# One layer of gated attention and SwiGLU in one kernel: transfers, short tiles and operand pieces put in another order

## The chip, the cores and the metric

The kernel runs on one core of a Trainium2 chip. The core has five engines that run their own instruction queues: TensorE (PE, with PEld for its weight loads), VectorE (DVE), ScalarE (ACT), GpSimd (POOL) and SyncE (SP), which here issues transfers and order marks. The metric is the device time of one execution in microseconds; less is better. Times given for a kernel are the median of several executions; the profile is one execution, profiled by hardware.

## The reference

The input x has 2048 rows of D = 640. One half of the result is attention with a memory, in H = 32 heads of 20 columns, over N = 4 chunks ("segments") of L = 512 rows, one after the other; the other half is a SwiGLU feed-forward with F = 1728. A gate of each row mixes them.

```python
for s in range(N):
    logits = einsum("bhqd,bhkd->bhqk", qs, ks) * scale + mask     # causal, within the chunk
    a_dot = softmax(logits) @ vs
    pq = phi(qs)                                                  # phi(t) = t + 1 or exp(t)
    a_mem = (pq @ M) / (pq @ z + 1e-6)
    o = g * a_mem + (1 - g) * a_dot                               # g = sigmoid(beta), per head
    M, z = M + phi(ks).T @ vs, z + sum(phi(ks))
a = concat(o) @ wo
b = (silu(x @ w1) * (x @ w3)) @ w2
out = gate * a + (1 - gate) * b                                   # gate = sigmoid(sum(x * gate_w))
```

All arrays are float32. The kernel keeps that precision in most products by splitting an operand into a high and a low part and adding three products.

## The kernel before, in words

The work on TensorE is of two kinds. Attention is written out slot by slot: 40 slots for each quad of four heads, and in fixed slots the units `s` (scores, for the row maximum, `s_unit`), `t` (transposed scores, for the exponential, `t_unit`) and once a quad `o` (probabilities times v, `pv_quad`). Everything else is a stream of dense tiles, objects of class `Work`, that fills the time between the units: q, k and v projections, memory tiles (pm, pkt, nd), the feed-forward's gate and up tiles (g, u), its down tiles (f), the output projection (op) and its normalization (rr, gt). A name such as `f0_13_2_1` is kind, chunk, group or block, row block and half of the columns. A dense tile takes one of TensorE's eight result banks from its first matmul until its evacuation: f tiles are added to the accumulator `acc` by VectorE (L775) or, for the first group, written by ScalarE (L773); op tiles are added by VectorE (L1063).

A dense tile is computed in two halves, of rows 0 to 63 and of rows 64 to 127 of the array (`halves`). The two halves use separate parts of the array, so the second half of one tile runs beside the first half of a later tile. For an order between them, SyncE runs a nop when the first half's last matmul is done, and the second half's first matmul waits for it:

```python
        if r == 0 and i == len(todo) - 1 and w.todo[1]:
            w.seen = order(nc.sync.nop(), ins)
        if r == 1 and i == 0 and w.todo[0]:
            order(ins, w.seen)
```

This nop (L203 in the profile) is the "order mark" below. It stands in SyncE's queue in the order in which the program was written, and so behind the transfers that were written before it and behind what these wait for.

What sets the order: TensorE's and SyncE's instructions stand as they were written; a scheduler places those of VectorE, ScalarE and GpSimd. A list of segments (`seg`) gives the dense tiles of a stretch of attention; `braid` lets a side stream give a tile every so many nanoseconds of a modelled clock, `chain` joins streams, and `step` chooses at each time whether the next matmul is one of a first half (`under`) or of the oldest second half (`behind_one`, `flight`). `after(n, f)` runs `f` n slots later.

The places that matter here:
- The end of each chunk c. The attention sums go to memory as `od` (from `oq`, by ScalarE's queue); `o_sums` reads their denominators back as `rs` (L895), `o_load` reads the rest as `oall` (L909, L911), `o_scale` has VectorE take reciprocals and split them in three bfloat16 parts `rp` (L915 to L920), and six transfers spread them as `rR` (L924). Tiles rr multiply `oall` by them; gt adds the memory's part, and `oproj` splits `oall` into `oT` (high and low part, by `split`: ScalarE L129 and VectorE or GpSimd L130) for the op tiles.
- The feed-forward has 13 blocks of 128 columns and a half block of 64 (number 13), in groups of which the last is `[13, 12]`. A down tile of that group is short: ten matmuls with 320 columns. Up tiles end in `ft` (VectorE L746) and its split `ht` (ScalarE L129, GpSimd L130), which the down tiles take.
- Between chunks 1 and 2 the inputs X2 and X3 are split (`split_x`, ScalarE and VectorE), and q, k and v of chunks 2 and 3 are projected. Weights come as `wr` (SyncE L340) and are split into `W` (ScalarE L129, GpSimd L130).

## Time and profile before

| quantity | value |
|---|---|
| median of 3 executions | 1202.81 us (1202.58 to 1205.58) |
| the profiled execution | 1202.51 us, span 1200.6 us |
| TensorE busy | 1127.3 us, 94% of the span |
| VectorE, ScalarE, GpSimd busy | 582.7, 483.8, 550.7 us |
| mean granted clock of TensorE | 0.974 |

The span runs from the first to the last instruction on the core; the time of an execution is a little longer. A busy share is taken over the whole span, while each stretch of the program has its own limit, so the stretches and the waits tell more than the totals. In rows of the profile `out<-in` are the program's names without their numbers, `x` a count, and the name behind `<-` in a wait is what ended it. SPq is SyncE's queue, where transfers and order marks stand.

### The profile page before, as it was taken

Reading aid. Unit: us, or ns where it says so; the run is one execution under the profiler, and the core shown is the slowest. Engines: PE = TensorE matmul, PEld = TensorE weight load, DVE = VectorE, ACT = ScalarE, POOL = GpSimd, SP = SyncE. Lnnn points to the kernel's source line nnn. Section 1 sums busy time; section 2 is a strip of 40 time slices with the busy share of each in tenths; the row PEclk is TensorE's granted clock in tenths of the full one; section 3 lists DMA queues with packets and bytes.
Section 4 is the critical chain, followed back from the end, with each engine's and each line's share of the span. In section 5 each row is a group of like instructions: output and inputs, shape, how many; then the busy total and the mean of one; then the engine's idle time right before and its main releaser. Section 6 shows DMA issues by size and latency. Waiting matters only on the chain.

```text
span 1200.6 us, 29765 instructions
## 1 busy us (share of the span) xinstructions
PE 1127.3 (94%) x11798; PEld 994.9 (83%) x11798; DVE 582.7 (49%) x1719; ACT 483.8 (40%) x988; POOL 550.7 (46%) x737
## 2 busy tenths in 40 slices
PE   9999999999999999869899979978998899998798
PEld 6998989888889889759798758877887778886797
DVE  5032654445456534542245567552557464552544
ACT  5254345553442433533455524435443344344040
POOL 5344355565553444233444435544664447554040
PEclk9999999999999999988999999999999999999899
DMA  8365743333433234234477853425542434442112
GB/s 287 114 225 178 255 133 79 88 111 87 133 90 87 68 87 129 92 94 128 150 247 219 271 160 95 132 78 150 162 118 57 112 77 126 121 130 62 34 34 88
DMA packets 86125, 152.66 MB, mean 127 GB/s; under 512 B 20068, under 2 KB 33124, under 8 KB 85988
## 3 DMA queue, kind: packets, MB, share of 16 engines
q1 hardware_dynamic: 55908, 94.50, 24.0%
q0 software_dynamic: 22880, 41.86, 14.3%
q10 hardware_dynamic: 7200, 14.42, 3.2%
q8 instruction: 93, 1.52, 0.5%
q14 instruction: 44, 0.36, 0.1%
HBM read 95.25 MB, written 54.53 MB: 125 GB/s over the span
## 4 chain that ended last, share of the span: by engine, by line
PE 82%; DVE 7%; ACT 4%; DMA 3%; issue 2%; SPq 2%; POOL 0%; DVEq 0%; ACTq 0%; POOLq 0%
PE u L200 15%; PE f L200 15%; PE g L200 14%; PE o L878 6%; PE v L200 6%; PE op L200 5%; PE q L200 5%; PE k L200 5%; PE t L860 4%; PE s L824 3%; DVE junk L833 2%; SPq L924 1%; PE pm L200 1%; PE nd L200 1%; ACT P L865 1%
## 5 line engine op out<-in xcount | busy, mean ns | idle before, releaser
L200 PE MATMUL g<-X,W 64*128 64x512 f32 x1680 | 387.6, 398 | 0.4 <-SPq L203 0.4
L200 PE MATMUL u<-X,W 64*128 64x512 f32 x1560 | 374.4, 398 | 12.8 <-SPq L203 12.7
L833 DVE CUSTOM_DVE_ANT_0 junk<-s,mask 128x128 bf16<-128x128 f32 (+3 forms) x512 | 250.9, 490 | 217.8 <-PE s L824 180.0
L130 POOL TENSOR_TENSOR W<-wr,W 128x640 fp32r<-128x640 f32 (+1 forms) x126 | 196.8, 1571 | 216.4 <-ACT W L129 193.9
L200 PE MATMUL f<-W,ht 64*128 64x320 f32 x2624 | 278.8, 317 | 16.9 <-SPq L203 8.2
L200 PEld LDWEIGHTS g<-X,W 64*128 64x128 f32 x1680 | 270.5, 187 | 13.2 <-issue 1.8
L200 PEld LDWEIGHTS u<-X,W 64*128 64x128 f32 x1560 | 257.4, 187 | 28.7 <-SPq L203 13.5
L200 PEld LDWEIGHTS f<-W,ht 64*128 64x128 f32 x2624 | 258.4, 192 | 25.5 <-SPq L203 8.8
L865 ACT ACTIVATE P<-t 128x384 f32<-128x384 f32 (+1 forms) x384 | 181.1, 527 | 200.1 <-PE t L860 191.5
L868 POOL TENSOR_SCALAR_AFFINE_SELECT P<-P 128x256 f32<-128x256 f32 (+1 forms) x192 | 95.2, 499 | 304.9 <-ACT P L865 291.8
L129 ACT CAST W<-wr 128x640 fp32r<-128x640 f32 (+1 forms) x131 | 92.9, 726 | 88.5 <-PE f L200 30.0
L200 PE MATMUL op<-W,oT 64*128 64x320 f32 x960 | 105.9, 313 | 6.4 <-ACT oT L129 3.7
L860 PE MATMUL t<-qk 62*128 62x256 f32 (+2 forms) x512 | 98.0, 340 | 10.0 <-DVE m L833 3.1
L200 PEld LDWEIGHTS op<-W,oT 64*128 64x128 f32 x960 | 94.9, 187 | 10.9 <-ACT oT L129 5.6
L775 DVE SCALAR_TENSOR_TENSOR acc<-f,cgate,acc 128x320 f32<-128x320 f32 x128 | 69.8, 549 | 67.4 <-PE f L200 66.6
L200 PE MATMUL k<-X,W 64*128 64x512 f32 x600 | 100.5, 405 | 0.0
L824 PE MATMUL s<-qk 60*128 60x256 f32 (+2 forms) x512 | 91.7, 330 | 5.9 <-ACT acc L773 3.1
L200 PE MATMUL q<-X,W 64*128 64x512 f32 x540 | 95.6, 403 | 0.1
L200 PE MATMUL v<-W,X 64*128 64x320 f32 (+1 forms) x960 | 85.4, 312 | 4.3 <-ACT W L129 3.2
L200 PEld LDWEIGHTS v<-W,X 64*128 64x128 f32 x960 | 82.9, 189 | 5.4 <-ACT W L129 3.5
L130 POOL TENSOR_TENSOR ht<-ft,ht 128x512 fp32r<-128x512 f32 x52 | 67.2, 1292 | 39.6 <-ACT ht L129 39.3
L860 PEld LDWEIGHTS t<-qk 62*128 62x128 f32 x512 | 64.2, 187 | 22.1 <-DVE m L833 5.0
(116 smaller groups left out, 1306.9 us busy)
## 6 DMA issues: line engine op xcount, KB each, us to landing
qk<-qkd POOLq DMA_DIRECT2D x128, 240.0 KB, 3.8
wr<-in_w_dram SPq DMA_DIRECT2D x80, 320.0 KB
qkd<-qs SPq DMA_DIRECT2D x20, 512.0 KB
qkd<-ks SPq DMA_DIRECT2D x20, 512.0 KB
od<-oq ACTq DMA_DIRECT2D x32, 256.0 KB
wr<-in_wo_dram SPq DMA_DIRECT2D x20, 320.0 KB
vg<-vd SPq DMA_DIRECT2D x16, 336.0 KB
xr<-in_xT_dram SPq DMA_DIRECT2D x20, 256.0 KB
```

The costliest lines, as they stand in the source:

```text
L129: pin(nc.scalar.copy(dst[:, 0], src))
L130: (lo or nc.gpsimd.tensor_sub)(dst[:, 1], src, dst[:, 0].bitcast(F32))
L200: ins = nc.tensor.matmul(o, l, x, start=i == 0 and (r == 0 or not w.todo[0]), stop=i == len(todo) - 1 and (r == 1 or not w.todo[1]), skip_ ...
L775: nc.vector.scalar_tensor_tensor(dst, ps[:, :320], cgate[:, c, lb:lb + 1], dst, op0=ALU.mult, op1=ALU.add)
L824: nc.tensor.matmul(ps[i][:, o:o + n], q[:, qb * P:(qb + 1) * P], k[:, :n], start=qb != 1, stop=qb != 0, skip_group_check=True)
L833: nc.vector.tensor_tensor_reduce(out=junk[:, :n], in0=ps[i][:, o:o + n], in1=mask[:, L - n:], scale=1.0, scalar=-3.0e38, op0=ALU.add, op1= ...
L860: nc.tensor.matmul(ps[i][:, o:o + L - q0], k[:, kb * P:(kb + 1) * P], q[:, q0:], start=kb != 2, stop=kb != 3, skip_group_check=True)
L865: last["exp"] = nc.scalar.activation(u["P"][:, i, o:o + n], ps[i][:, b:b + n], AF.Exp, scale=SCALE)
L868: nc.gpsimd.affine_select(d, d, pattern=[[0, 2], [0, n], [1, P]], base=0, channel_multiplier=-1, compare_op=ALU.is_ge, fill=0.0)
L878: nc.tensor.matmul(ps[32 * i:32 * i + 32, kb * P:], heads[2 * p + i]["v"][:, kb], pairs[p + i // 2]["P"][:, i % 2, o:o + n], start=kb == 0 ...
L924: after(3 - i if c < NSEG - 1 else 2, lambda d=dst, s=rp[4 * h0:4 * h0 + 4 * n, i]: here(nc.sync.dma_start(d, s)))
```

## The change

The kernel does the same arithmetic. What differs is order:
- `rs`, `oall` and `rR` transfers of a chunk's end get slots of their own: one `oall` each second slot, `rR` from the third slot on, one a slot (for the last chunk one each second slot, and every second one of them goes to GpSimd's queue). `o_scale` follows `rs` after 8 slots instead of 10 (after 5 instead of 3 for the last chunk).
- A tile can name a condition (`ready`): a down tile, that `ht` exists; an op tile, that its `oT` exists. The stream holds tiles back in `waiting` until no first half is under way, and until no more than three second halves are left behind; otherwise `lower` runs matmuls of second halves alone. Sides and timed tiles, too, wait for fewer than three second halves.
- The last group of the feed-forward is cut by chunk: f0_13 runs as a side of u1 and then alternates with the splits of X2; the first four tiles of f1_13 run beside the store of chunk 0's result, the others as a side of v2, with X3's splits as another side. In the tail f2_13 stands right behind the up tiles, and op3 alternates with f3_13.
- `oT` is split in two pieces, of two and three blocks of 128 columns' length, instead of one.
- q's projections for the first block of chunks 2 and 3 come behind K's. Weights have a lower bound (`floors`), so that one still needed by the other chunk isn't given up.
- Stores of q, k and memory parts come a slot or two later; chunks 2 and 3 are stored block by block by `store_block`.

```diff
@@ step, pull
-                open_work(y)
+                waiting.append(y)
                 return True
...
+            elif n > 8 and lower():
+                return True
...
+    def lower():
+
+        if flight[0] is None:
+            dense["n0"] += APART
+            if not follow():
+                return False
+        w = flight[0]
+        if one(1, w):
+            flight[0] = None
+            close_work(w)
+        return True
...
-            elif dense["ns"] >= d.due and len(under) < 2:
+            elif dense["ns"] >= d.due and len(under) < 2 and len(behind_one) < 3:
...
-        elif under:
+        elif not under and waiting and (len(behind_one) > 3 or waiting[0].ready is not None and not waiting[0].ready()):
+            if not lower():
+                raise RuntimeError("nothing makes " + waiting[0].name + " ready")
+        elif under or waiting:
+            if not under:
+                open_work(waiting.popleft())
@@ ffn_down
-            return Work(f"f{c}_{js[0]}_{lb}_{hf}", parts, evac, 800, idx[0])
+            return Work(f"f{c}_{js[0]}_{lb}_{hf}", parts, evac, 800, idx[0], None, lambda: all((c, j) in hts for j in js))
@@ pv_quad, o_sums, o_load, o_scale
-            after(6 if c < NSEG - 1 else 2, o_sums, c)
+            after(6, o_sums, c)
...
-        after(10 if c < NSEG - 1 else 3, o_scale, c)
-        if c == NSEG - 1:
-            o_load(c, KB - 1)
-        else:
-            after(6, o_load, c, KB - 1)
+        after(8 if c < NSEG - 1 else 5, o_scale, c)
+        after(6 if c < NSEG - 1 else 2, o_load, c, KB - 1)
...
+        for i, (h, e, n, r) in enumerate(rows(b)):
+            src = od[c][h:h + n // DH, :DH] if n > DH else od[c][h, e:e + n]
+            after(1 + 2 * i, lambda d=oall[c][r:r + n, b], s=src: here(nc.sync.dma_start(d, s)))
...
+        end = c == NSEG - 1
         for i in range(3):
-            for base, h0, n in ((0, 0, R1H + 1), (64, R1H, H - R1H)):
+            for k, (base, h0, n) in enumerate(((0, 0, R1H + 1), (64, R1H, H - R1H))):
                 dst = rR[base + n * i:base + n * i + n].rearrange("h (a n) -> h a n", n=P)
-                after(3 - i if c < NSEG - 1 else 2, lambda d=dst, s=rp[4 * h0:4 * h0 + 4 * n, i]: here(nc.sync.dma_start(d, s)))
-        after(8, turned.append, c)
+                queue = nc.gpsimd if end and k else nc.sync
+                after(3 + 2 * i if end else 3 + 2 * i + k,
+                      lambda d=dst, s=rp[4 * h0:4 * h0 + 4 * n, i], q=queue: here(q.dma_start(d, s)))
+        after(11, turned.append, c)
@@ oproj
-            split(oT[0][:, qb % 2].rearrange("p a (b n) -> p a b n", n=P), oall[c][:, :, qb * P:(qb + 1) * P],
-                  lo=nc.vector.tensor_sub)
+            for b0, b1 in ((0, 2), (2, KB)):
+                split(oT[0][:, qb % 2].rearrange("p a (b n) -> p a b n", n=P)[:, :, b0:b1],
+                      oall[c][:, b0:b1, qb * P:(qb + 1) * P], lo=nc.vector.tensor_sub)
@@ the list of segments
+    def alternate(a, b):
+
+        def gen():
+            for y in a[1]:
+                yield y
+                z = next(b[1], None)
+                if z is not None:
+                    yield z
+            yield from b[1]
+        return a[0] + b[0], gen()
...
-    seg += [(0, load_raw(2)), (0, load_raw(3))] + u0 + [braid(chain(u1), (0, x2), 2800, 4500, False)]
-    d = job_down(A, 4)
-    q = job_q(B[:1], 0, {2: big_tile})
-    seg += [braid(chain([braid(braid(d, (0, store(0)), 2600, 12000), (0, x2), 5300)] + q), (0, x3), 4000, 13000)] + job_v(B)
-    seg += jobs_k(B) + job_q(B[1:], 0, {3: slot})
+    d0, d1 = jobs_down_by_chunk(A, 4)
+    v2, v3 = job_v(B)
+    seg += [(0, load_raw(2)), (0, load_raw(3))] + u0
+    seg += [braid(braid(chain(u1), (0, x2), 1900, 4200, False), d0, 2600, 2500, False), alternate(d0, (0, x2))]
+    seg += [braid(take(d1, 4), (0, store(0)), 700), braid(braid(v2, d1, 2400), (0, x3), 3000, 2000), v3]
+    seg += jobs_k(B)
+    q = job_q2(B, 0, {2: big_tile, 3: slot})
+    seg += q[:2]
...
-    tail = [braid(chain([d] + u), o1, 1500, 10500)] + [o2, job_down(B, 4, True)]
+    tail = [braid(chain([d] + u + [d2]), o1, 1500, 10500), alternate(o2, d3)]
```

VectorE's order where the short down tiles of chunk 0 are evacuated (`acc0<-f0_13_...`; X2 is the split of chunk 2's input, junk and m are row maxima of attention, fu and ft are of an up tile). Before:

```order
L775 SCALAR_TENSOR_TENSOR acc0_2778<-f0_13_0_0_7610,cgate_101,acc0_2778 128x320
L307 TENSOR_TENSOR X2_7512<-xr2_7245,xh2_4_7724 128x512
L775 SCALAR_TENSOR_TENSOR acc0_2778<-f0_13_0_1_7629,cgate_101,acc0_2778 128x320
L775 SCALAR_TENSOR_TENSOR acc0_2778<-f0_13_1_0_7649,cgate_101,acc0_2778 128x320
L775 SCALAR_TENSOR_TENSOR acc0_2778<-f0_13_1_1_7659,cgate_101,acc0_2778 128x320
L775 SCALAR_TENSOR_TENSOR acc0_2778<-f0_13_2_0_7669,cgate_101,acc0_2778 128x320
L307 TENSOR_TENSOR ns0_98<-m48_7084,nh24_7797 128x16
L844 STREAM_TRANSPOSE mr_7801<-ns0_98 32x32 x4
L775 SCALAR_TENSOR_TENSOR acc0_2778<-f0_13_2_1_7679,cgate_101,acc0_2778 128x320
L775 SCALAR_TENSOR_TENSOR acc0_2778<-f0_13_3_0_7701,cgate_101,acc0_2778 128x320
L775 SCALAR_TENSOR_TENSOR acc0_2778<-f0_13_3_1_7717,cgate_101,acc0_2778 128x320
```

And now, from the third of these tiles on:

```order
L758 SCALAR_TENSOR_TENSOR fu1_12_7666<-ft1_12_7665,g1_12_7492 128x512
L809 SCALAR_TENSOR_TENSOR acc0_2776<-f0_13_1_0_7603,cgate_101,acc0_2776 128x320
L775 SCALAR_TENSOR_TENSOR ft1_12_7665<-fu1_12_7666,u1_12_7586 128x512
L809 SCALAR_TENSOR_TENSOR acc0_2776<-f0_13_1_1_7649,cgate_101,acc0_2776 128x320
L869 ISA junk_7752,m48_7132<-s25_2_0_7748,mask_85 128x512
L869 ISA m48_7132 128x1
L869 ISA junk_7754,m48_7132<-s25_2_1_7749,mask_85 128x512
L869 ISA m48_7132 128x1
L809 SCALAR_TENSOR_TENSOR acc0_2776<-f0_13_2_0_7678,cgate_101,acc0_2776 128x320
L809 SCALAR_TENSOR_TENSOR acc0_2776<-f0_13_2_1_7690,cgate_101,acc0_2776 128x320
L809 SCALAR_TENSOR_TENSOR acc0_2776<-f0_13_3_0_7710,cgate_101,acc0_2776 128x320
L809 SCALAR_TENSOR_TENSOR acc0_2776<-f0_13_3_1_7730,cgate_101,acc0_2776 128x320
```

Before, the tiles stood one behind the other; now two steps of the up tile 12 of chunk 1 and row maxima of another pair lie among them, and X2's split has moved ahead.

VectorE's order at the end of chunk 2, up to where `o_scale` makes `rp` from `rs`. Before:

```order
L775 SCALAR_TENSOR_TENSOR acc3_11984<-f3_3_3_0_13511,cgate_101,acc3_11984 128x320
L833 ISA junk_13650,m100_13360<-s51_0_0_13644,mask_85 128x128
L833 ISA m100_13360 128x1
L833 ISA junk_13652,m100_13360<-s51_0_0_13644,mask_85 128x256
L833 ISA m100_13360 128x1
L833 ISA junk_13654,m100_13360<-s51_0_1_13645,mask_85 128x128
L833 ISA m100_13360 128x1
L833 ISA junk_13656,m100_13360<-s51_0_1_13645,mask_85 128x256
L833 ISA m100_13360 128x1
L915 RECIPROCAL rs_95<-rs_95 128x128
L775 SCALAR_TENSOR_TENSOR acc3_11984<-f3_3_3_1_13554,cgate_101,acc3_11984 128x320
```

And now:

```order
L809 SCALAR_TENSOR_TENSOR acc3_12012<-f3_3_2_1_13478,cgate_101,acc3_12012 128x320
L945 RECIPROCAL rs_95<-rs_95 128x128
L946 TENSOR_SCALAR rs_95<-rs_95,cR_93 128x128
L947 CAST rp_96<-rs_95 128x128
L869 ISA junk_13653,m100_13355<-s51_0_0_13647,mask_85 128x128
L869 ISA m100_13355 128x1
L948 TENSOR_TENSOR rs_95<-rs_95,rp_96 128x128
L869 ISA junk_13655,m100_13355<-s51_0_0_13647,mask_85 128x256
L869 ISA m100_13355 128x1
L949 CAST rp_96<-rs_95 128x128
```

The reciprocal stood behind the evacuation of f3_3_3_0 and the first row maxima of pair 51 (s51); now it stands ahead of both, right behind f3_3_2_1.

SyncE's order at the end of chunk 3, from `rs` on (order marks are not among these rows). Before:

```order
L895 DMA rs_95<-od3_79 128x1x128
L911 DMA oall3_15601<-od3_79 8x512
L909 DMA oall3_15601<-od3_79 120x1x512
L924 DMA rR_97<-rp_96 20x4x128
L924 DMA rR_97<-rp_96 13x4x128
L924 DMA rR_97<-rp_96 20x4x128
L924 DMA rR_97<-rp_96 13x4x128
L924 DMA rR_97<-rp_96 20x4x128
L924 DMA rR_97<-rp_96 13x4x128
L340 DMA wr128_16430<-in_wo_dram 128x640
```

And now:

```order
L931 DMA rs_95<-od3_79 128x1x128
L941 DMA oall3_15616<-od3_79 8x512
L941 DMA oall3_15616<-od3_79 120x1x512
L957 DMA rR_97<-rp_96 20x4x128
L369 DMA wr127_16445<-in_wo_dram 128x640
L957 DMA rR_97<-rp_96 20x4x128 x2
L369 DMA wr128_16506<-in_wo_dram 128x640
L369 DMA wr129_16874<-in_wo_dram 128x640
```

Three of the six `rR` are left here, with loads of wo between them; the other three stand in GpSimd's queue. At the end of chunk 2 the six still stand one behind the other among SyncE's transfers.

87 lines of the change are left out of this document (55 added, 32 removed).

## The prediction

> **What bounds the kernel now.** I read the page first, for the span and for who is busy, then the stretches of 20 to 30 us, to find where TensorE does less than elsewhere, then TensorE's waits, and last the queue of SyncE and the chain at each hole.
>
> ```profile
> span 1200.6 us, 29765 instructions
> PE 1127.3 (94%) x11798; PEld 994.9 (83%) x11798; DVE 582.7 (49%) x1719; ACT 483.8 (40%) x988; POOL 550.7 (46%) x737
> ```
>
> The second line makes TensorE the bound, and no other engine is busy for half of the span. Since the change leaves all matmuls in place, it can only win what TensorE loses. In the stretches below (start:end, length, then busy us and number of instructions for PE, PEld, DVE, ACT, POOL, then the granted clock) I compare numbers of matmuls, since a busy PE may be a slow one.
>
> ```profile
> 360.00:380.00 20.00, 18.70 (x236) 17.70 (x235) 13.96 (x43) 3.14 (x8) 4.44 (x8) 1.00 0.23 68
> 390.00:420.00 30.00, 30.00 (x306) 25.32 (x304) 16.37 (x48) 12.46 (x24) 13.67 (x13) 1.00 0.24 69
> 450.00:480.00 30.00, 30.00 (x380) 28.61 (x380) 14.76 (x41) 9.44 (x20) 14.78 (x20) 1.00 0.45 126
> 480.00:510.00 30.00, 26.17 (x231) 23.50 (x219) 16.11 (x46) 14.86 (x27) 8.64 (x8) 0.94 0.28 95
> 510.00:540.00 30.00, 20.36 (x171) 16.97 (x171) 13.94 (x30) 12.06 (x23) 10.71 (x17) 0.83 0.32 94
> 540.00:570.00 30.00, 28.95 (x343) 27.19 (x345) 8.50 (x33) 9.04 (x23) 9.18 (x16) 0.89 0.40 124
> 690.00:720.00 30.00, 22.47 (x206) 17.40 (x204) 17.69 (x55) 8.30 (x17) 10.93 (x15) 0.91 0.50 160
> 720.00:750.00 30.00, 29.98 (x291) 24.55 (x289) 21.13 (x63) 14.30 (x31) 16.91 (x23) 0.98 0.33 91
> 750.00:780.00 30.00, 30.00 (x357) 25.66 (x356) 16.86 (x55) 12.32 (x26) 17.45 (x27) 1.00 0.51 135
> 780.00:810.00 30.00, 23.98 (x270) 21.08 (x268) 16.23 (x58) 9.90 (x20) 12.12 (x16) 0.94 0.25 74
> 810.00:840.00 30.00, 26.91 (x304) 23.74 (x304) 8.96 (x37) 16.09 (x34) 12.98 (x23) 0.94 0.51 148
> 920.00:940.00 20.00, 13.49 (x114) 11.70 (x111) 11.52 (x35) 7.00 (x15) 7.60 (x9) 0.83 0.31 93
> 1110.00:1120.00 10.00, 2.92 (x22) 2.92 (x24) 2.99 (x8) 0.62 (x1) 2.62 (x2) 0.69 0.15 36
> ```
>
> Full stretches give the price of a matmul: 30.00/380 = 79 ns where the short ones (64x320) prevail, 30.00/306 = 98 ns and 29.98/291 = 103 ns where the long ones (64x512) do, 30.00/357 = 84 ns for a mixture. Length less number times price is what each hole loses:
> - A, 480 to 570 (the short down projection of chunks 0 and 1): 30 - 231 x 0.098 = 7.4, 30 - 171 x 0.079 = 16.5, 30 - 343 x 0.079 = 2.9: 26.8 us.
> - B, 690 to 720 (end of chunk 1): 30 - 206 x 0.103 = 8.8.
> - C, 780 to 840 (output projection of chunk 1, then f2_0): 60 - 574 x 0.084 = 11.8.
> - D, 920 to 940 (end of chunk 2): 20 - 114 x 0.103 = 8.3.
> - E, 1110 to 1120 (end of chunk 3): 10 - 22 x 0.079 = 8.3.
> - end of chunk 0, 360 to 380: 20 - 236 x 0.079 = 1.4.
>
> Together 65.4 us. TensorE's waits (total, times, longest) say what ends them:
>
> ```profile
> PE u L200 <- SPq L203: 12.7, 3, 6.5
> PE f L200 <- SPq L203: 8.2, 2, 8.0
> PE f L200 <- DVE acc L775: 5.0, 5, 2.1
> PE op L200 <- ACT oT L129: 3.7, 7, 0.7
> PE s L824 <- ACT acc L773: 3.1, 1, 3.1
> PE op L200 <- DVE oT L130: 2.7, 6, 1.1
> ```
>
> The first two are TensorE waiting for SyncE's order mark (the nop between a tile's halves), which stands in SyncE's queue behind transfers. They are B, D and E. The third is A: 16 tiles of ten matmuls in all eight banks, each opened when VectorE has emptied an old one.
>
> **The change part by part.** Spaced transfers first. SyncE's timeline and the chain show what it stands behind at each end:
>
> ```profile
> 368.25 5.23 SPq L924 DMA_DIRECT2D rR<-rp  x6
> 705.49 0.58 SPq L895 DMA_DIRECT2D rs<-od  x1
> 927.85 5.07 SPq L924 DMA_DIRECT2D rR<-rp  x6
> 1111.83 5.13 SPq L924 DMA_DIRECT2D rR<-rp  x6
> ```
> ```profile
> 699.18 6.29 DMA od<-oq
> 807.06 8.34 DMA wr<-in_w_dram
> 1107.06 3.18 DMA rs<-od
> ```
>
> One rR costs 5.07/6 = 0.85 us of SyncE's time. At the end of chunk 3 (E) the order of after puts one rs, one oall and then an order mark, and the rR come singly, with three given to GpSimd. So neither the landing of rs nor the six issues stand before the marks of f2_9. Of 8.3 us I take 8.0, since one issue of 0.85 can still show; bounds 6 (a mark behind two transfers and a cold clock) and 9 (the slow matmuls around it too). GpSimd's three issues stand among its splits of wo's weights, which aren't asked for before the tail: at nothing, but without that cover the weights, and op with them, come 3 x 0.85 us later. At D all six rR are still together in SyncE's order, but VectorE's scaling, for which SyncE stands at this end today, comes some 2 us of TensorE's work sooner, and the mark behind the six, of u2_6, is needed 5.5 us after the one ahead. (Distances in TensorE's work are counted in the orders: matmuls between, times the prices above.) 6 x 0.85 = 5.1 just fits, and the fifth is needed by the normalization matmul. I take 6 of 8.3, bounds 3 and 8. At B three rR stand ahead of the mark of u3_0 instead of two, but VectorE's scaling comes earlier; rs still waits for the 6.29 us of od's landing, which nothing in the change shortens. I take 3 of 8.8, bounds 0 and 7. End of chunk 0: the 5.23 us are spread over several marks, 1.0 of 1.4, bounds 0 and 1.4.
>
> Short tiles, A. In the order of after the second halves stay about four tiles behind instead of seven, and other tiles, x2's splits and v2 lie between. A bank is then asked for 0.9 to 1.8 us of TensorE's work after its VectorE step begins, which the 0.55 us below fits into. What is late next is the first tile of each set: f0_13 opens right behind u0_12, f1_13 behind u1_12, so each waits for the three steps that make ht (line, engine, operation, tiles; busy us, mean ns):
>
> ```profile
> L129 ACT CAST W<-wr 128x640 fp32r<-128x640 f32 (+1 forms) x131 | 92.9, 726 | 88.5 <-PE f L200 30.0 <-PE u L200 23.1 <-PE op L200 12.9
> L746 DVE SCALAR_TENSOR_TENSOR ft<-fu,u 128x512 f32<-128x512 f32 x52 | 35.6, 685 | 30.7 <-PE u L200 30.2
> L129 ACT CAST ht<-ft 128x512 fp32r<-128x512 f32 x52 | 32.3, 621 | 55.3 <-DVE ft L746 53.2 <-DMA od<-oq 2.1
> L130 POOL TENSOR_TENSOR ht<-ft,ht 128x512 fp32r<-128x512 f32 x52 | 67.2, 1292 | 39.6 <-ACT ht L129 39.3
> L775 DVE SCALAR_TENSOR_TENSOR acc<-f,cgate,acc 128x320 f32<-128x320 f32 x128 | 69.8, 549 | 67.4 <-PE f L200 66.6
> ```
>
> 0.685 + 0.621 + 1.292 = 2.6 us. Between lie 0.6 us of work for f0_13 (2.0 late) and 1.5 for f1_13, where one cast of a weight (0.726) stands ahead on ScalarE (1.8 late). Such a stall also slows what follows:
>
> ```profile
> 502.27 0.38 PE L860 MATMUL t<-qk 62*128 62x256 f32 x1 [2.13 <-DVE m L833]
> 504.79 0.62 PE L200 MATMUL u<-X,W 64*128 64x512 f32 x1
> 506.37 0.39 PE L200 MATMUL u<-X,W 64*128 64x512 f32 x1
> ```
>
> After 2.13 us without work a matmul takes 0.62 instead of 0.39 us until 506.4, so four us at little over half speed: at most 2 us lost, at least none; I take 1.2 for a stall of two. New losses 2.0 + 1.8 + 2 x 1.2 = 6.2, and 2 more for v's weights and x3's splits, which share the engines: 26.8 - 8.3 = 18.5 gained. Bounds 8 (half of the lock-step stays with the new stalls) and 24. The Trainium skill, "TensorE: Matmul & The Clock Gate", section "Why this matters for your kernels", sets the limit for keeping the full clock at idle gaps of about 3 us. By that rule stalls of 2 us cost no clock, and three of them would be 3.6 us cheaper, 1158 instead of 1162; the row of 502.27 speaks against it, with the reservation that another short wait follows there.
>
> q behind K moves q's first projections of chunks 2 and 3 behind the K tiles. The matmuls are the same; their stores come to SyncE's queue later, and the load of pair 16 that reads them stands 12 us of TensorE's work behind. Another 12 are left till the first s unit, which cover the landing below: at nothing; without that cover the unit waits for a load, 3.8 us.
>
> ```profile
> qk<-qkd POOLq DMA_DIRECT2D x128, 240.0 KB, 3.8
> ```
>
> Operand in pieces. A piece of 256 or 384 columns takes less than the whole 640, so the first op matmul waits for roughly half as long; the waits are 3.7 + 2.7 = 6.4 us. In the tail op3 and f3_13 also alternate, which gives each piece a tile's time. I take 4.5, bounds 2 and 6.4; the 32 added casts and subtractions lie on engines that are idle for half of the span. Against it stands the tail's new first tile: f2_13 follows u2_12 after 0.15 us of work, so 2.6 - 0.15 = 2.4 late and 1.2 of clock. Net 0.9, bounds -1.6 and 5. C also holds a weight that comes late (8.34 us in flight, with ScalarE's cast ahead of the evacuations that TensorE's s unit waits 3.1 us for). That cast's place hardly moves, so I take 3 of 11.8, bounds 0 and 8. The limit on sides (a memory tile only when fewer than three halves are behind) and the later store slots move work that has slack: nothing.
>
> Sum: 18.5 + 3 + 3 + 6 + 8 + 0.9 + 1.0 = 40.4. The profiled execution took 1202.51, as good as the median of 1202.81: 1202.5 - 40.4 = 1162. The low ends sum to 8 + 0 + 0 + 3 + 6 - 1.6 + 0 = 15 (1187), the high ones to 24 + 7 + 8 + 8 + 9 + 5 + 1.4 = 62 (1140).
>
> **Rivals.**
> The stalls only move. If ht's three steps and the dense VectorE keep A at its low end, the tail too, and B and C give nothing: 8 + 6 + 8 - 1.6 + 1 = 21, 1181. For it speaks that A's tiles, splits and ht share three engines; against, that VectorE is busy for 13.94 of 30 us there.
> All holes close: 1140. For it, that every hole has an edit; against, od's 6.29 us and the weight's 8.34, which none shortens.
> The spacing isn't there: the six rR stay together at the ends of chunks 1 and 2, and if the marks still fall behind them, B and D give nothing: 40.4 - 9 = 31.4, 1171. The order speaks for it, the marks' places against it.
> Slower: the scaling of the sums (o_scale) comes two slots sooner, and VectorE works in order.
>
> ```profile
> DVE rs L915 <- DMA rs<-od: 3.3, 1, 3.3
> ```
>
> If its reciprocal is now reached while rs is in flight, VectorE stands, and all evacuations with it. The longest flight would be od and rs, 6.29 + 0.58 + 3.18 = 10 us. At four chunk ends that is 40 us, and the gains at the ends (18) don't come: 1202.5 - 22.4 + 40 = 1220. It decides from 22.4/4 = 5.6 us a stop. Against it: today VectorE stands there once, for 3.3 us, with TensorE idle anyway.
>
> **How the numbers follow.** My forecast (1152 to 1170) has 0.40, the moved stalls 0.20, the missing spacing 0.12, all holes closed 0.15, the stop of VectorE 0.10, and 0.03 is left for gains and stops that cancel. A change is measurable from 0.3%, 3.6 us: faster 0.87, same 0.03, slower 0.10. The range 1141 to 1188 takes in the bounds and all but the last two cases.
>
> **What would show it.** After: no wait of u or f for the order mark over 2 us at the ends of chunks 2 and 3; A's stretches with over 300 matmuls in 30 us and no row of five waits for acc; instead two or three waits of f for ht near 2 us, one in the tail; op's waits under 3 us. The prediction fails if VectorE waits for rs more than 5 us an end, if a new wait for weights or qk appears in A, or if C's late weight costs more than now.

## The result and the profile after

| kernel | median | lowest to highest | against before |
|---|---|---|---|
| before | 1202.81 us | 1202.58 to 1205.58 | |
| after | 1165.18 us | 1160.91 to 1166.93 | 0.9673 (95%: 0.9627 to 0.972) |

The change wins 38 us. The profiled execution of after took 1166.93 us, the longest of its three. The page's first lines, as for before:

```profile
span 1165.2 us, 29806 instructions
PE 1113.2 (96%) x11798; PEld 993.9 (85%) x11798; DVE 584.9 (50%) x1735; ACT 485.8 (42%) x1003; POOL 551.4 (47%) x739
```

TensorE ran the same 11798 matmuls and was busy for 14 us less; its mean granted clock was 0.990 instead of 0.974. Some stretches of after, with the columns of the prediction's stretches (by the milestones below, the same work stands 5 us later than before at A, 13 us earlier at B and 19 us earlier at D):

```profile
480.00:510.00 30.00, 24.31 (x218) 20.15 (x216) 13.90 (x31) 14.59 (x26) 9.99 (x10) 0.97 0.43 135
510.00:540.00 30.00, 26.89 (x288) 24.71 (x287) 16.16 (x42) 13.33 (x29) 14.99 (x25) 0.92 0.34 98
540.00:570.00 30.00, 30.00 (x404) 28.33 (x402) 10.77 (x42) 10.88 (x30) 5.72 (x9) 1.00 0.31 105
690.00:720.00 30.00, 26.50 (x243) 22.24 (x241) 19.40 (x62) 11.26 (x23) 17.36 (x25) 1.00 0.56 153
900.00:920.00 20.00, 19.18 (x172) 15.35 (x173) 13.60 (x40) 8.15 (x17) 12.55 (x17) 1.00 0.53 128
1080.00:1090.00 10.00, 8.81 (x114) 8.53 (x112) 6.99 (x13) 1.35 (x2) 5.00 (x6) 1.00 0.37 101
```

The two holes behind the order marks, D (now from 900 on) and E (now near 1085), are nearly closed: 172 matmuls in 20 us and 114 in 10, where before held 114 and 22. B (690 to 720) is smaller. A is the surprise: at 510 the count rose from 171 to 288, but 480 to 510 holds 218 where before held 231. TensorE's waits in after (total, times, longest):

```profile
PE t L896 <- ACT acc L807: 3.3, 2, 2.9
PE f L201 <- POOL ht L130: 3.3, 3, 1.6
PE f L201 <- ACT ht L129: 2.8, 2, 1.4
PE pm L201 <- SPq L204: 2.4, 1, 2.4
PE f L201 <- DVE acc L809: 2.2, 2, 1.2
PE op L201 <- DVE oT L130: 1.9, 2, 1.4
PE g L201 <- SPq L204: 1.7, 1, 1.7
```

The 12.7 and 8.2 us for order marks are gone. Of the five waits of f for acc two are left, both far behind the short tiles (at 886 and 1010); among the short tiles an s unit now waits for acc instead, 1.8 us at 507. The waits of f for ht are the first tiles of the short sets. Two waits for an order mark are new: that of a memory tile (pm) in the head, and that of a gate tile (g) in A. At the end of chunk 2 the six rR still come together in SyncE's queue, and VectorE's wait for rs is small:

```profile
904.29 5.44 SPq L957 DMA_DIRECT2D rR<-rp  x6
```
```profile
DVE rs L945 <- DMA rs<-od: 5.4, 2, 3.5
```

To see where the time went I use a milestone that all kernels share: the start of ScalarE's copy of a quad's attention sums. There are 32 of them, eight a chunk, counted from 0, and the quads' attention is the same in all kernels, so the time between two of them goes by the dense tiles woven in. Two such rows of after, of quads 9 and 12:

```profile
443.52 0.59 ACT L919 COPY oq<-o 128x512 f32<-128x512 f32 x1 [2.81 <-PE o L914]
589.32 0.59 ACT L919 COPY oq<-o 128x512 f32<-128x512 f32 x1 [4.62 <-PE o L914]
```

Their difference, 145.8 us, is the second line of this table; the other lines are worked out in the same way, and the last column is what the prediction had for the holes that lie there.

| stretch | what it holds | before | after | gained | predicted |
|---|---|---|---|---|---|
| to quad 9 | head, end of chunk 0 | 438.5 | 443.5 | -5.0 | 1.0 |
| 9 to 12 | A, the short tiles | 152.7 | 145.8 | 6.9 | 18.5 |
| 12 to 15 | K, q and memory tiles of chunks 1 to 3 | 107.4 | 96.5 | 10.9 | nothing |
| 15 to 16 | B, end of chunk 1 | 33.4 | 28.7 | 4.7 | 3 |
| 16 to 23 | C, op of chunk 1, f2_0 | 181.4 | 180.2 | 1.2 | 3 |
| 23 to 24 | D, end of chunk 2 | 32.3 | 26.2 | 6.1 | 6 |
| 24 to 31 | op of chunk 2, feed-forward | 158.7 | 155.6 | 3.1 | part of 0.9 |
| from 31 | E, end of chunk 3, the tail | 96.2 | 88.7 | 7.5 | 8, part of 0.9 |
| sum | span | 1200.6 | 1165.2 | 35.4 | 40.4 |

A tile that was moved can change stretches, so the first three don't hold quite the same work. TensorE's matmuls and mean granted clock in them, before and after:

| stretch | matmuls before | after | clock before | after |
|---|---|---|---|---|
| to quad 9 | 4480 | 4506 | 1.00 | 1.00 |
| 9 to 12 | 1486 | 1498 | 0.93 | 0.98 |
| 12 to 15 | 976 | 931 | 0.97 | 1.00 |

At some 0.1 us a matmul, for the same work the head lost about 2.4 us instead of 5.0 (pm's new wait is 2.4), the short tiles gained about 8 instead of 6.9, and the stretch from 12 to 15 about 6.4 instead of 10.9.

The ends of the chunks came out near the forecast. The short tiles gave 7 or 8 of 18.5, and a place where the prediction saw nothing gave 6 to 11.

### The profile page after: what moved, and what is told of

Same layout as the page of the kernel before. It is cut to its first block, busy times and chain, and to the rows that moved or that the text cites. A ratio compares the mean times of both kernels' runs of the same rounds, so it can differ in the third digit from the quotient of the medians.

```text
span 1165.2 us, 29806 instructions
## 1 busy us (share of the span) xinstructions
PE 1113.2 (96%) x11798; PEld 993.9 (85%) x11798; DVE 584.9 (50%) x1735; ACT 485.8 (42%) x1003; POOL 551.4 (47%) x739
## 5 line engine op out<-in xcount | busy, mean ns | idle before, releaser
L201 PE MATMUL g<-X,W 64*128 64x512 f32 x1680 | 383.2, 397 | 2.5 <-SPq L204 1.7
L201 PE MATMUL u<-X,W 64*128 64x512 f32 x1560 | 363.6, 397 | 1.8 <-ACT P L901 1.0
L201 PEld LDWEIGHTS g<-X,W 64*128 64x128 f32 x1680 | 266.5, 186 | 14.4 <-SPq L204 2.1
L201 PEld LDWEIGHTS u<-X,W 64*128 64x128 f32 x1560 | 253.7, 186 | 13.2 <-issue 2.0
L201 PE MATMUL q<-X,W 64*128 64x512 f32 x540 | 88.6, 396 | 0.0
L201 PE MATMUL v<-W,X 64*128 64x320 f32 (+1 forms) x960 | 82.7, 307 | 0.6 <-DVE acc L809 0.6
L201 PEld LDWEIGHTS k<-X,W 64*128 64x128 f32 x600 | 80.7, 187 | 2.2 <-issue 0.2
```

Source lines behind the costliest of these rows:

```text
L201: ins = nc.tensor.matmul(o, l, x, start=i == 0 and (r == 0 or not w.todo[0]), stop=i == len(todo) - 1 and (r == 1 or not w.todo[1]), skip_ ...
```

## The experiments

Twelve kernels were run, each timed against before on the same chip. All compute the whole result. The first table has their times; the second, from the one profiled execution of each, the length of six stretches in us. The profiles scatter with the executions (old_short and tail_order, whose instructions are the same up to there, differ by 4.5 us between quads 18 and 20), so the second table tells places, and the first one sizes.

| kernel | median us (range) | against before (95%) |
|---|---|---|
| old_transfers | 1190.79 (1189.38 to 1192.57) | 0.990 (0.9843 to 0.9956) |
| only_transfers | 1181.34 (1179.84 to 1183.47) | 0.9822 (0.9766 to 0.9878) |
| old_short | 1151.9 (1150.74 to 1152.45) | 0.9574 (0.9509 to 0.9638) |
| one_piece | 1172.26 (1170.99 to 1177.46) | 0.9753 (0.9694 to 0.9812) |
| no_limit | 1183.09 (1180.93 to 1187.52) | 0.9825 (0.98 to 0.985) |
| only_limit | 1178.79 (1176.91 to 1182.87) | 0.9789 (0.9767 to 0.9811) |
| old_short_q | 1164.42 (1160.68 to 1169.48) | 0.9667 (0.9632 to 0.9703) |
| combined | 1159.35 (1156.87 to 1160.55) | 0.962 (0.9604 to 0.9637) |
| tail_order | 1146.29 (1140.33 to 1150.6) | 0.9521 (0.9475 to 0.9566) |
| combined_held | 1158.72 (1157.68 to 1159.34) | 0.9625 (0.9585 to 0.9664) |
| limit_transfers | 1159.23 (1158.24 to 1159.69) | 0.9631 (0.9598 to 0.9663) |
| combined_vector | 1156.13 (1153.51 to 1159.92) | 0.9584 (0.9542 to 0.9626) |

| kernel | to 9 | 9 to 12 | 12 to 15 | 15 to 16 | 23 to 24 | from 31 |
|---|---|---|---|---|---|---|
| before | 438.5 | 152.7 | 107.4 | 33.4 | 32.3 | 96.2 |
| after | 443.5 | 145.8 | 96.5 | 28.7 | 26.2 | 88.7 |
| old_transfers | 443.7 | 145.1 | 96.6 | 33.5 | 36.9 | 96.3 |
| only_transfers | 436.1 | 151.5 | 107.5 | 28.7 | 27.0 | 88.7 |
| one_piece | 444.3 | 146.5 | 96.6 | 28.6 | 26.2 | 88.8 |
| no_limit | 443.4 | 153.4 | 102.5 | 28.4 | 30.1 | 88.8 |
| only_limit | 437.9 | 138.7 | 107.5 | 33.4 | 32.4 | 96.1 |
| limit_transfers | 436.9 | 137.3 | 106.4 | 26.5 | 28.8 | 86.5 |
| old_short | 439.7 | 136.3 | 98.4 | 27.4 | 25.6 | 86.8 |
| old_short_q | 440.8 | 141.8 | 101.6 | 27.3 | 29.9 | 86.9 |
| tail_order | 437.5 | 135.9 | 98.4 | 27.1 | 25.6 | 83.6 |
| combined | 434.0 | 137.1 | 107.0 | 26.6 | 31.6 | 85.7 |
| combined_held | 434.1 | 138.3 | 107.5 | 27.9 | 31.6 | 85.3 |
| combined_vector | 434.1 | 138.3 | 109.9 | 26.5 | 31.2 | 85.6 |

### The transfers: undone alone, done alone

old_transfers is after with the transfers of the chunks' ends as before:

```diff
-            after(6, o_sums, c)
+            after(6 if c < NSEG - 1 else 2, o_sums, c)
...
-        after(8 if c < NSEG - 1 else 5, o_scale, c)
-        after(6 if c < NSEG - 1 else 2, o_load, c, KB - 1)
+        after(10 if c < NSEG - 1 else 3, o_scale, c)
+        if c == NSEG - 1:
+            o_load(c, KB - 1)
+        else:
+            after(6, o_load, c, KB - 1)
...
+                after(3 - i if c < NSEG - 1 else 2, lambda d=dst, s=rp[4 * h0:4 * h0 + 4 * n, i]: here(nc.sync.dma_start(d, s)))
-        after(11, turned.append, c)
+        after(8, turned.append, c)
```

> The changed kernel with the sums, the reads of oall and the rR transfers at the chunk ends placed as before; all else as changed. Theory (the gains belong to places and add up): the losses at the ends of chunks 1, 2 and 3 and 0 come back, between the two profiles about 5 + 8 + 8 + 1.7 = 23 us, so about 1187 us (1180 to 1193), with waits of u and f for the order mark of 5 to 8 us at the ends of chunks 2 and 3. Rival (the limit of second halves, or other tiles at these places, made the gain): not above 1172 us, and no wait for the order mark above 3 us.

only_transfers is the other way round: before, with the new code of `pv_quad`, `o_sums`, `o_load` and `o_scale`.

> The kernel before with only the new placing of the sums, the reads of oall and rR. Theory: it wins the same as the run above loses, about 20 us, so 1183 us (1178 to 1190), and the short tiles' hole at 500 to 548 us stays as it was. Rival (the waits only move, VectorE stands for rs instead): 1195 us or more, with VectorE's reciprocal waiting for rs more than 5 us at each of three ends.

Measured: 25.6 us over after, and 1.8% (21 us) under before. The three stretches of chunks' ends carry it in both directions (33.5 and 28.7, 36.9 or 32.3 and 27, 96.3 and 88.7). TensorE's waits in old_transfers have the order marks back, and at chunk 2 a wait for the transfer itself:

```profile
PE f L201 <- SPq L204: 8.1, 2, 7.8
PE rr L201 <- DMA rR<-rp: 7.1, 1, 7.1
PE u L201 <- SPq L204: 6.5, 1, 6.5
```

So the gain of the new placing as a whole is shown, and it hardly depends on the other parts. Which piece of it acts at which end (the slots of `rR`, those of `oall`, the earlier `o_scale`, GpSimd's queue) was not tried. B gave more than the prediction's 3 of 8.8: 4.7 both times.

### The limit of second halves: undone alone, done alone

no_limit is after without the limit in the main stream; sides and timed tiles keep theirs.

```diff
-        elif not under and waiting and (len(behind_one) > 3 or waiting[0].ready is not None and not waiting[0].ready()):
+        elif not under and waiting and (len(behind_one) > 30 or waiting[0].ready is not None and not waiting[0].ready()):
```

> The changed kernel without the limit of four second halves in the main stream (the readiness, the woven order and the limit on sides stay). New theory (the limit, not the weave, frees the result banks in time for the short tiles): the waits of f for acc come back in the stretch of the short tiles, 1172 to 1185 us. Rival (other tiles between the short ones are enough): 1165 us, within 4.

only_limit is before with `waiting`, `lower` and the limits of four (stream) and three (sides, timed tiles), without conditions of readiness and with the short tiles back to back as they were:

```diff
@@ before: pull, events, step
-                open_work(y)
+                waiting.append(y)
...
-            if dense["ns"] >= e[0] and len(under) < 2:
+            if dense["ns"] >= e[0] and len(under) < 2 and len(behind_one) < 3:
...
+        elif not under and waiting and len(behind_one) > 3:
+            if not lower():
+                raise RuntimeError("no second half")
```

> The kernel before with only the two limits of second halves (main stream and sides); order of tiles, transfers and pieces as before. New theory: the short tiles' hole closes about as far as with the old order in the changed kernel, 25 us between ScalarE's copies of the attention sums of quads 9 and 15 (260 us before, 235 there): 1178 us (1172 to 1186), with the holes at the chunk ends as before. Rival (the limit needs the new order or q behind K): 1192 us or more.

Measured: without the limit 18 us over after; the limit alone takes 2.1% (25 us) from before. A's stretch from 510 on, first in no_limit, then in only_limit, and then TensorE's waits between quads 9 and 12: for the accumulator in before and in only_limit, and the three longest rows for f in no_limit:

```profile
510.00:540.00 30.00, 22.96 (x192) 20.47 (x189) 14.62 (x39) 9.49 (x19) 11.96 (x19) 0.79 0.26 84
```
```profile
510.00:540.00 30.00, 27.27 (x313) 23.46 (x313) 17.31 (x42) 16.41 (x34) 19.27 (x31) 1.00 0.56 170
```
```profile
PE f L200 <- DVE acc L775: 4.7, 4, 2.1
```
```profile
PE f L200 <- DVE acc L794: 0.3, 2, 0.2
```
```profile
PE f L201 <- POOL ht L130: 3.0, 2, 2.2
PE f L201 <- ACT ht L129: 2.8, 2, 1.4
PE f L201 <- DVE acc L809: 1.9, 1, 1.9
```

The limit without the weave brings A from 152.7 to 138.7 us and takes f's waits for acc away: it is enough to break the lock-step between TensorE's banks and VectorE. The weave without the limit leaves A at 153.4, but not with the waits of before: f waits 1.9 us for acc instead of 4.7 (and an s unit 1.8), and 5.8 for ht have come. no_limit also has q behind K, which by the next section costs 5.5 us in this stretch, so what the short tiles' weave gains alone was not measured.

The two runs met their expectations in the time, but not everywhere in the place. Of no_limit's 18 us the profiles put 7.6 in A, 6.0 between quads 12 and 15 and 3.9 at the end of chunk 2. only_limit was to win 25 us between quads 9 and 15 and wins 13.9 there; 7.0 more lie between 16 and 23, a stretch that scatters.

### The short tiles back to back, and q's place

old_short is after with the old order of this stretch: short tiles back to back, q of chunk 2 between them and v, q of chunk 3 after K. Limits, transfers and pieces are those of after.

```diff
-    v2, v3 = job_v(B)
...
-    seg += [braid(take(d1, 4), (0, store(0)), 700), braid(braid(v2, d1, 2400), (0, x3), 3000, 2000), v3]
-    seg += jobs_k(B)
-    q = job_q2(B, 0, {2: big_tile, 3: slot})
-    seg += q[:2]
+    d = d0[0] + d1[0], (y for _, g in (d0, d1) for y in g)
+    seg += [(0, load_raw(2)), (0, load_raw(3))] + u0 + [braid(chain(u1), (0, x2), 2800, 4500, False)]
+    q = job_q(B[:1], 0, {2: big_tile})
+    seg += [braid(chain([braid(braid(d, (0, store(0)), 2600, 12000), (0, x2), 5300)] + q), (0, x3), 4000, 13000)] + job_v(B)
+    seg += jobs_k(B) + job_q(B[1:], 0, {3: slot})
...
-    seg = q[2:] + job_q(B, 2)
+    seg = job_q(B, 1) + job_q(B, 2)
```

> The changed kernel, with the stretch between the up tiles of the last group of chunks 0 and 1 and K of chunks 2 and 3 as before: all 16 short down tiles back to back, q of chunk 2 ahead of v, q of chunk 3 behind K; the limit of second halves stays. Theory (the weaving makes the gain): the hole comes back by the 12 us that the profiles differ there, about 1177 us (1172 to 1184), with several waits of f for VectorE's acc. Rival (the limit of four second halves alone frees the banks in time): 1165 to 1169 us.

It should have been slower than after, and is 13 us faster (the executions lie far apart, 1152.45 at most and 1160.91 at least; the intervals of the two ratios still overlap by 0.001). So either the weave or q's place costs time. old_short_q tells them apart: old_short, but q behind K as in after (the diff is against old_short).

```diff
-    q = job_q(B[:1], 0, {2: big_tile})
-    seg += [braid(chain([braid(braid(d, (0, store(0)), 2600, 12000), (0, x2), 5300)] + q), (0, x3), 4000, 13000)] + job_v(B)
-    seg += jobs_k(B) + job_q(B[1:], 0, {3: slot})
+    seg += [braid(braid(braid(d, (0, store(0)), 2600, 12000), (0, x2), 5300), (0, x3), 4000, 13000)] + job_v(B)
+    seg += jobs_k(B)
+    q = job_q2(B, 0, {2: big_tile, 3: slot})
+    seg += q[:2]
...
-    seg = job_q(B, 1) + job_q(B, 2)
+    seg = q[2:] + job_q(B, 2)
```

> As old_short (the 16 short tiles back to back), but q of chunk 2 stays behind K as in the changed kernel. If the weave is what costs 13 us, the time stays with old_short's, 1152 us (1148 to 1156). If q behind K is what costs, it goes most of the way back, 1158 to 1166 us, with new waits between K and q.

Its ratio is that of after (0.9667 and 0.9673): the weave as such gives nothing measurable. Against old_short, q's place costs 0.0093 x 1202.8 = 11 us; the two ran on different chips, and their intervals just overlap. The profiles put it at 5.5 between quads 9 and 12, 3.2 between 12 and 15 (where 987 matmuls stand instead of 969, worth some 1.8), and 4.3 at the end of chunk 2. The stretch from 510 on in old_short, then in old_short_q, and then two stalls of TensorE in old_short_q's timeline:

```profile
510.00:540.00 30.00, 27.23 (x313) 23.50 (x313) 17.25 (x41) 16.39 (x33) 19.29 (x31) 1.00 0.57 170
```
```profile
510.00:540.00 30.00, 25.56 (x262) 21.64 (x259) 15.19 (x32) 13.73 (x27) 16.30 (x27) 0.83 0.38 115
```
```profile
523.88 0.63 PE L201 MATMUL v<-W,X 64*128 64x320 f32 x1 [2.31 <-DVE acc L809]
529.02 0.80 PE L896 MATMUL t<-qk 62*128 62x256 f32 x3 [1.76 <-DVE X L331]
```

Behind the short tiles come q's long matmuls in old_short, and v's short ones in old_short_q. v's first tile then asks for a bank that VectorE has not yet emptied, and a little later attention waits while VectorE splits X. With q between them neither wait is there. Between quads 9 and 12 the mean granted clock is 0.95 instead of 0.99, worth some 5 of the 5.5 us; the waits themselves, 2.3 and 1.8 us, stand against 1.2 for a weight and 1.2 for acc in old_short. The 4.3 us at the end of chunk 2 have a wait of TensorE for `rp` in the trace, 2.7 us, with the cause described under combined below; how q's place leads there was not tried.

### The operand in pieces

one_piece is after with `oT` split whole.

```diff
-            for b0, b1 in ((0, 2), (2, KB)):
-                split(oT[0][:, qb % 2].rearrange("p a (b n) -> p a b n", n=P)[:, :, b0:b1],
-                      oall[c][:, b0:b1, qb * P:(qb + 1) * P], lo=nc.vector.tensor_sub)
+            split(oT[0][:, qb % 2].rearrange("p a (b n) -> p a b n", n=P), oall[c][:, :, qb * P:(qb + 1) * P],
+                  lo=nc.vector.tensor_sub)
```

> The changed kernel with oT split as a whole again. Theory: op's waits for oT (1.9 us in the profile of the changed kernel, 6.4 before) return where op tiles stand back to back, for chunks 0, 1 and 2 but not in the tail, where f3_13 lies between: 3 us, so 1168 us (1165 to 1171). Rival (the pieces cost as much in instructions as they win): 1165 us or less.

Measured: 7 us over after, a little above the expected range; the intervals of the two ratios overlap, so the pieces' gain is not clear of the scatter. TensorE's waits for the operand in one_piece, beside the single row of 1.9 us in after:

```profile
PE op L201 <- DVE oT L130: 3.4, 6, 1.3
PE op L201 <- ACT oT L129: 3.3, 4, 1.5
```

6.7 - 1.9 = 4.8 us of these waits are not in after, near the 4.5 of the prediction; the rest of the 7 is not placed.

### Two parts alone, together

limit_transfers is before with the edits of only_limit and of only_transfers.

> The kernel before with the limits of second halves and the new placing of the chunk-end transfers, nothing else. Theory (two separate places, so the gains add): 1203 - 25 - 22 = 1156 us (1152 to 1161). Rival (each changes when the dense tiles fall among the attention units, so the other's gain is partly lost): 1164 us or more.

Measured 0.9631, 44 us under before (0.0369 x 1202.8): nearly the 25 and 21 of the two alone. These two parts give at least as much as the whole change, which has 38 (the intervals overlap).

### Looking for the best: the tail's order, and old due times

tail_order is old_short with the last group's up tiles in another order, g and u of block 12 for chunk 2 ahead of those for chunk 3 (g2, u2, g3, u3 instead of g2, g3, u2, u3), so that u2_12, which the first short down tile needs, ends one tile earlier:

```diff
-    d, u = job_down(B, 3), [job_up(B, j, j < NF) for j in GROUPS[4]]
+    d, u = job_down(B, 3), [job_up(B, j) for j in GROUPS[4]]
```

> old_short with only the order g2, u2, g3, u3 of the last up tiles (the combined kernel without the old due times of memory tiles and stores). Theory (in combined the due times cost the 8 us, by what then falls together at the ends of chunks 1 and 2): 1150 us (1148 to 1152), with 25 to 26 us between the attention copies of quads 23 and 24 as in old_short. Rival (the order of the up tiles costs): 1157 us or more, most of it behind quad 31.

combined is the same kernel but for four numbers, which it takes from before: how late memory tiles are due, and how many slots later stores are issued.

```diff
-    def store_later(dst, src, key=None, queue=nc.sync, n=5):
+    def store_later(dst, src, key=None, queue=nc.sync, n=4):
...
-                store_later(gd[c][:, qb, 320 * hf:320 * hf + 320], gm, ("g", c, qb, hf), n=4)
+                store_later(gd[c][:, qb, 320 * hf:320 * hf + 320], gm, ("g", c, qb, hf), n=2)
...
-                timed.append((dense["ns"] + 3400, lambda: memory_turn(c, mb)))
+                timed.append((dense["ns"] + 2800, lambda: memory_turn(c, mb)))
...
-            timed.append((dense["ns"] + 1900, lambda: memory_write(c, mb)))
+            timed.append((dense["ns"] + 1400, lambda: memory_write(c, mb)))
```

> old_short, with the last two up tiles in the order g2, u2, g3, u3, so that u2_12 ends one tile earlier ahead of f2_13, and with the memory tiles' and stores' old due times. Theory: the opener's stall in the tail (1.43 + 0.85 us and the slow clock behind it, 4.6 us lost in ten) goes, and the wait of pm for the order mark (2.4 us) in the first 90 us: 1152 - 4 - 3 = 1145 us (1142 to 1149). Rival (u3_12's end is then what the tail waits for, the memory tiles lose as much elsewhere): 1150 us or more.

tail_order has the lowest median of all, 4.8% under before, a little below its expected range and clearly under after. Against old_short its gain is inside the scatter (the intervals overlap); in the profiles the tail is 3.2 us shorter (86.8 and 83.6), and the opener's stall of 1.43 and 0.84 us in old_short is gone. combined was to win the 3 us that after loses in the head, where its first memory tile waits for an order mark. It wins 3.5 there (434.0 and 437.5) and is still 13 us slower than tail_order (12 by the ratios, whose intervals lie apart). Between quads 12 and 15 every kernel with the old numbers needs 106 to 110 us, every one with the new numbers 96 to 103. TensorE's waits there in before (591 to 699), in combined (571 to 678) and in tail_order (573 to 672):

```profile
PE pkt L198 <- DVE pk L492: 3.7, 1, 3.7
PE nd L200 <- DVE gm L567: 2.2, 1, 2.2
```
```profile
PE pkt L199 <- DVE pk L521: 2.2, 1, 2.2
PE nd L201 <- DVE gm L596: 1.8, 1, 1.8
PE u L201 <- DVE nd_r L594: 1.7, 1, 1.7
```
```profile
PE nd L201 <- DVE pq L521: 1.1, 1, 1.1
PE t L896 <- DVE gm L596: 1.1, 1, 1.1
```

With the memory tiles called 500 to 600 ns later on the planner's clock, TensorE waits 2.2 us in these rows instead of 5.7. tail_order and combined differ in the four numbers alone, so the 8.6 us between them in this stretch (107.0 and 98.4, with 980 and 969 matmuls) are theirs, but for the scatter. after has the new numbers as well, so the greater part of its 10.9 us here is due to them and to the 45 matmuls that stand elsewhere, and not to the short tiles; the wait of pkt for pk is still in after, 1.8 us at 584, just ahead of quad 12. Which of the four numbers does it was not tried.

### combined's lost time at the end of chunk 2

Between quads 23 and 24 combined needs 31.6 us, tail_order 25.6. In combined's trace three steps of `o_scale` on VectorE are five times as long as in tail_order's (0.29, 0.23 and 0.29 us), beside splits of weights on GpSimd. The timeline of VectorE there, and GpSimd's row:

```profile
888.48 1.44 DVE L946 TENSOR_SCALAR rs<-rs,cR 128x128 f32<-128x128 f32 x1
890.18 1.25 DVE L947 CAST rp<-rs 128x128 bf16<-128x128 f32 x1
891.57 1.44 DVE L948 TENSOR_TENSOR rs<-rs,rp 128x128 f32<-128x128 f32 x1
```
```profile
888.26 4.59 POOL L130 TENSOR_TENSOR W<-wr,W 128x640 fp32r<-128x640 f32 x3 [0.93 <-ACT W L129]
```

combined_held was to keep these splits away from the place:

```diff
-        elif raws and raws[0][0] < clock["oldest"] + NW and \
+        elif raws and not clock.get("hold") and raws[0][0] < clock["oldest"] + NW and \
...
+        clock["hold"] = c in (2,)
...
+        after(9, lambda: clock.update(hold=False))
```

> The combined kernel, with GpSimd's splits of wo's weights held back from the issue of rs of chunk 2 until nine slots behind o_scale. In combined VectorE's six steps from rs to rp took 6.77 us there, beside 4.66 us of GpSimd's splits, and 2.45 to 2.86 us wherever no split ran. Theory (VectorE's steps wait for GpSimd's subtraction of two operands): the six steps take under 3.5 us, rR starts 3 to 4 us sooner, and 31.6 us between the attention copies of quads 23 and 24 become 26 to 28: 1154 to 1156 us. Rival (the steps are long for another reason, or TensorE waits for the held weights instead): 1159 us or more.

It decided nothing: 0.9625, and its splits overlapped the steps as before. combined_vector gives the three splits to VectorE instead:

```diff
-        split(w[:, :, :n], raw[:, :n], lo=nc.vector.tensor_sub if k < 7 else None, pin=behind(after))
+        split(w[:, :, :n], raw[:, :n], lo=nc.vector.tensor_sub if k < 7 or k in (104, 105, 106) else None, pin=behind(after))
```

> The combined kernel, with the three weights of wo that GpSimd splits beside o_scale of chunk 2 (4.66 us of overlap there, in combined and in combined_held alike) split by VectorE instead, where they stand between o_scale's steps. Theory (VectorE's small steps wait for GpSimd's subtraction of two operands): with GpSimd not subtracting there, the steps of rs and rp take 0.2 to 0.3 us each again (reciprocal 0.95), against 1.44, 1.25 and 1.44 us. The three splits add about 1 us each between them, so from the reciprocal to the last rp it is still 5 to 6 us, and the time falls little: 1155 to 1159 us. Rival (the steps are long for a reason of VectorE's own): they stay above 1 us each, and the time is 1161 us or more.

With GpSimd idle the same steps, and one of the three splits, in combined_vector:

```profile
893.75 0.28 DVE L946 TENSOR_SCALAR rs<-rs,cR 128x128 f32<-128x128 f32 x1
893.95 0.82 DVE L130 TENSOR_TENSOR W<-wr,W 128x640 fp32r<-128x640 f32 x1
895.03 0.23 DVE L947 CAST rp<-rs 128x128 bf16<-128x128 f32 x1
896.57 0.28 DVE L948 TENSOR_TENSOR rs<-rs,rp 128x128 f32<-128x128 f32 x1
```

The cause of the long steps is thereby shown. That they cost the time isn't shown by this run: from the reciprocal's start to the last step's end it takes 6.55 us (892.74 to 899.29) instead of 6.78, since VectorE now does the splits between the steps, and the stretch is 31.2 us instead of 31.6. The median is 3 us under combined's, with overlapping intervals.

The other traces say more. TensorE's two longest waits between quads 23 and 24 of combined are these; in tail_order none there is over 0.2 us:

```profile
PE u L201 <- SPq L204: 2.1, 1, 2.1
PE g L201 <- DVE m L869: 1.5, 1, 1.5
```

The mark that u waits for stands in SyncE's queue behind the six rR, and the first of these starts when the first `rp` is done: 4.0 us behind the reciprocal's start in combined (891.47), 1.6 us in tail_order (883.89). The row maximum m stands among the long steps. Behind the second wait the granted clock is 0.50 for 4 us.

In the eleven kernels with the new transfers the length of the stretch goes roughly with the time from the reciprocal's start to the last `rp`. Where the splits start when most steps are done (after, one_piece, old_short, tail_order) this is 4.1 us, and the stretch 25.6 to 26.2. Where they fall among the steps, or VectorE does them, it is 5.1 to 7.2 us, and the stretch 27.0 to 31.6 (only_transfers, limit_transfers, old_short_q, no_limit and the three combined kernels). In old_short_q and no_limit TensorE waits there 2.7 us for `rp` and 2.2 us for an evacuation behind it, again with a clock of 0.50 for the next 4 us. So where GpSimd's splits fall is the likely cause of this stretch's 6 us. No run moved only the splits out of the way, so it is not shown.

## Why the prediction was right, and where it was not

The time was forecast as 1162 and is 1165.18; the case that came true is the forecast's own. That the sum came out within 4 us is partly luck: A gave 11.6 us less than its term, a stretch that the sum had at nothing gave 10.9 more, and these two errors cancel. (A's new losses of 2.0, 1.8, 2.4 and 2 add up to 8.2, not 8.3, which changes nothing.)

**The ends of the chunks were right.** B, D and E were 3, 6 and 8, measured 4.7, 6.1 and, with the tail, 7.5; only_transfers has the last 7.5 too, without the new tail. B was sized too low: od's flight is still there (rs is issued 5.0 us behind od, 6.3 before), but TensorE waits for no order mark at that place any more. The rival without spacing at chunk 2 fell although its ground was true: the six rR do stand together (5.44 us), but TensorE waits for no mark meanwhile. The stop of VectorE fell too: 5.4 us in two waits, where its price began at 5.6 for each end.

**"18.5 gained" for A was wrong in its size and in its cause.** Of 18.5 the stretch gave 6.9, and over 300 matmuls in 30 us, as the prediction wanted of all of A, are found in one of its three stretches. The step "the second halves stay about four tiles behind instead of seven, and other tiles lie between" names two causes as one. The runs show that the limit alone clears the lock-step (152.7 to 138.7); the weave with q behind K, but without the limit, leaves the stretch as long as it was (153.4). The bounds of 8 and 24 held the limit's worth of 14, and hardly that of the change, 7 or 8. What the sum for A lacked stands in after's trace: 1.7 us for an order mark, 1.8 us of an s unit for acc with a granted clock of 0.53 from 508.0 to 511.4 behind it, and q's place.

**"At nothing" for q behind K was wrong.** The prediction looked for who reads q later, and found cover for that. It didn't ask what q's long matmuls had covered where they stood: the emptying of the short tiles' banks and X's splits. That costs about 11 us, half of it in A.

**"Work that has slack: nothing" was wrong.** It was said of the limit on sides and the later stores; the due times of the memory tiles, which the change moves too (the list of its parts leaves them out), were not looked at at all. The four later numbers cost 3.5 us in the head and win some 12 in the whole (tail_order against combined).

**The first tiles of the short sets** were to be late by 2.0, 1.8 and 2.4 us, each with 1.2 of clock. TensorE's timeline of after has them at f0_13 (two rows), f1_13 and f2_13 (two rows):

```profile
498.31 0.41 PE L201 MATMUL f<-W,ht 64*128 64x320 f32 x1 [1.41 <-ACT ht L129]
499.67 0.41 PE L201 MATMUL f<-W,ht 64*128 64x320 f32 x1 [0.80 <-POOL ht L130]
...
521.94 4.10 PE L201 MATMUL f<-W,ht 64*128 64x320 f32 x32 [1.60 <-POOL ht L130]
...
1124.74 0.55 PE L201 MATMUL f<-W,ht 64*128 64x320 f32 x2 [1.43 <-ACT ht L129]
...
1126.15 0.63 PE L201 MATMUL f<-W,ht 64*128 64x320 f32 x1 [0.85 <-POOL ht L130]
```

That is 2.21, 1.60 and 2.28. The granted clock (the number before the last two) behind the second and third:

```profile
521.94:526.04 4.10, 4.10 (x34) 4.10 (x35) 1.66 (x3) 0.00 (x0) 0.61 (x2) 0.60 0.27 80
1127.00:1130.00 3.00, 3.00 (x24) 3.00 (x22) 0.00 (x0) 0.00 (x0) 0.00 (x0) 0.60 0.00 0
```

4.10 x 0.40 = 1.6 us and 3.00 x 0.40 = 1.2 us are lost there; behind f0_13's, which comes in two pieces, the clock stays at 1.00. The limit of about 3 us of idle in the Trainium skill, "TensorE: Matmul & The Clock Gate", section "Why this matters for your kernels", does not hold here as a bound: the clock fell behind waits of 1.60 us (521.94) and 1.78 us (507.11). No shorter limit follows from this: in the same trace it stayed at 1.00 behind waits of 1.70 us (482.52), 1.78 us (584.38) and 1.90 us (699.37), and old_short has f2_13's stall of 1.43 and 0.84 us with the clock at 1.00 behind it. What decides is open, so 1.2 us of clock for each stall was a guess that came true at two of three.

**The pieces** were 4.5, of waits 4.8. **C** gave 1.2 of 3, less than the scatter of this stretch: old_short and tail_order, whose instructions are the same up to the last group of up tiles, need 59.4 and 54.9 us between quads 18 and 20, and what differs is a wait for an evacuation by ScalarE, 2.3 us in the one and 0.6 in the other, with a clock of 0.50 behind the longer one.

The parts do not add up exactly. Limits and transfers make 1159.23; with the pieces, the tail's order and the rest of after's code but the old due times, combined is at 1159.35. The pieces' 7 us, measured in the company of the new due times, are not seen there. This stays open.
